# Stage three of a long convolution from cosine and sine sums: four plain float32 matmuls a step in place of twelve float32r ones

## The chip, the cores and the metric

The kernel runs on one core of a Trainium2 chip. The metric is the device time of one execution in microseconds (us); the profile's times are from the first to the last instruction of one profiled execution. The engines are TensorE (PE; PEld are its weight loads), VectorE (DVE), ScalarE (ACT), GpSimd (POOL) and SyncE (SP), which issues most of the DMAs.

## The reference

A gated long convolution and then a feed-forward layer, on 4 sequences of 12480 tokens with 128 channels:

```python
h_mlp = np.maximum(pos_emb @ w1, 0.0) @ w2
h_filt = h_mlp * np.exp(-0.01 * pos)[:, None]
u = x * v
y = irfft(rfft(u, n=2 * S, axis=1) * rfft(h_filt, n=2 * S, axis=0), n=2 * S, axis=1)[:, :S]
a = (x * y).reshape(B * S, D)
h = np.maximum(a @ w_in, 0.0)
out = h * h @ w_out
```

Here S is 12480, B 4, D 128, and the hidden width of the feed-forward layer 2048.

## The kernel before

**The convolution as a two-level transform.** The sequence is padded to 112 x 112 (I = 112) and transformed in two levels with tables of cosines and sines. Stage one multiplies x and v and transforms along the first index for each channel; stage two applies the second level, multiplies with the transform of the filter and keeps the products in W; stage three does the first level of the way back; stage four the second level, multiplies by x and writes the result, transposed, to DRAM (zd), from where the feed-forward layer reads it. W is one SBUF tile of 56 x 512 values a partition: 128 channels, and 4 values for each channel and row pair. Every stage of every batch works in it in place.

**Stage three** runs 64 steps of two channels. In a step, `prep` (L420) casts the pair's 448 values a partition out of W into `vh` as float32r (L424, ScalarE), `prep2` (L427) subtracts it to get the low part `vl` (L431, VectorE), `mm` (L434) makes for each channel k and each part r (real, imaginary) three float32r matmuls through `mm3` (L78 to L80: high x high, high x low, low x high) of 224 columns against the table `ft`, so that r = 0 and r = 1 accumulate into one result, and `evac` (L444) copies the 448 results back into the same channels of W (L445, ScalarE). The table holds the values for an index m and its mirror 111 − m side by side, real and imaginary, split in high and low: 4 x 224 values a partition, loaded by GpSimd's DMA queue (`load_tab`, L84).

**The order of the work** is written out by hand. Each stage is a generator that yields 1, 2 or 3. For batch 0 the stages run by themselves (`big` is true): stage three then prepares two steps ahead and copies back two steps late, and after each step the hook `during` runs one piece of `convert_weights`, which turns 64-bit weights into float32r pairs on VectorE and ScalarE (L113 to L132). For batches 1 to 3 the four stages are one stream, and the feed-forward loop at the end of the kernel advances it: `adv(1)` before its first matmuls, `adv(2)` before ScalarE's work, `adv(3)` after VectorE's. So one step of a stage goes with one feed-forward step f: 6 matmuls into A (L78 to L80), 6 into O for the step before last (`m_o` runs while more than one low part is pending), on ScalarE relu (L686) and square (L693), on VectorE the cast of the square (L700) and the subtraction that gives its low part gl (L705). Every eighth step GpSimd splits a new input (L653).

**Buffers.** PSUM has two pairs of banks A (`psa`), three single banks F (`bank()`, `psf`) and one O. Stage three of batches 1 to 3 takes one F bank a step.

Of the kernel before, what the change touches and what calls it, by code (L numbers as in the profile page):

```python
# [7 lines left out]
F32 = mybir.dt.float32  # L8
F32R = mybir.dt.float32r
# [8 lines left out]
I = 112  # L18
S = I * I
# [3 lines left out]
NP = I // 2  # L23
# [6 lines left out]
HI = I // 2  # L30
# [5 lines left out]
def hyena_moe_kernel(  # L36
# [19 lines left out]
    nc = tc.nc  # L56
# [4 lines left out]
    psa = ctx.enter_context(tc.tile_pool(name="psa", bufs=2, space=bass.MemoryType.PSUM))  # L61
# [3 lines left out]
    W = cpool.tile([KP, NP, 4 * D], F32, name="W")  # L65
# [6 lines left out]
    def bank():  # L72
        return psf.tile([128, 512], F32, tag="F", name="F")

    def mm3(o, L, R, first=True, last=True):
        lh, ll = L
        rh, rl = R
        nc.tensor.matmul(o, lh, rh, start=first, stop=False)  # L78
        nc.tensor.matmul(o, lh, rl, start=False, stop=False)  # L79
        nc.tensor.matmul(o, ll, rh, start=False, stop=last)  # L80

    def load_tab(p, src, k):
        t = p.tile([I, k, 2 * I], F32R, name="tab", bufs=1)
        nc.gpsimd.dma_start(out=t, in_=src)  # L84
        return t

    def convert_weights(p, tp, dst):
        n = 512
# [49 lines left out]
    def by_channel(d0, d1):  # L138
        return W[:I].rearrange("p t (d c) -> p d t c", c=4)[:, d0:d1]
# [199 lines left out]
    def stage2(filt, big, side="left", hook=None):  # L339
# [6 lines left out]
        with pool("s2", side) as p:  # L346
# [51 lines left out]
            for t in range(n + lag):  # L398
# [9 lines left out]
                if hook is not None:  # L408
                    hook(t)

    def stage3(big, ft=None, hook=None):
        n = D // 2
        with pool("s3") as p:
            if ft is None:
                ft = load_tab(p, f_tab, 4)
            q = {}
            pa = 2 if big else 1
            lag = 2 if big else 1

            def prep(t):  # L420
                if t >= n:
                    return
                hi = p.tile([I, 2, NP, 4], F32R, tag="vh", name="vh", bufs=lag + pa)
                nc.scalar.copy(hi, by_channel(2 * t, 2 * t + 2))  # L424
                q[t] = hi

            def prep2(t):  # L427
                if t >= n:
                    return
                lo = p.tile([I, 2, NP, 4], F32R, tag="vl", name="vl", bufs=lag + pa)  # L430
                nc.vector.tensor_sub(out=lo, in0=by_channel(2 * t, 2 * t + 2), in1=q[t].bitcast(F32))  # L431
                q[t] = q[t], lo

            def mm(t):  # L434
                hi, lo = q.pop(t)
                A = bank()
                for k in range(2):
                    o = A[:I, k * 2 * I : (k + 1) * 2 * I]
                    for r in range(2):
                        h, l = (x[:, k].rearrange("p t (k r) -> p (t k) r", r=2)[:, :, r] for x in (hi, lo))  # L440
                        mm3(o, (h, l), (ft[:, 2 * r, :], ft[:, 2 * r + 1, :]), first=r == 0, last=r == 1)
                return A

            def evac(t, A):  # L444
                nc.scalar.copy(by_channel(2 * t, 2 * t + 2), A[:I, : 4 * I].rearrange("p (d t c) -> p d t c", d=2, c=4))  # L445

            if not big:
                yield from rest(2)
            yield 1
            for t in range(pa):  # L450
                prep(t)
            yield 2
            for t in range(pa):
                prep2(t)
            prev = {}
            for t in range(n + lag):
                yield 1
                if t - lag in prev:
                    evac(t - lag, prev.pop(t - lag))
                prep(t + pa)  # L460
                yield 2
                prep2(t + pa)
                yield 3
                if t < n:
                    prev[t] = mm(t)
                if hook is not None:
                    hook(t - n)
# [129 lines left out]
    ftp = take("ftp")  # L597
# [17 lines left out]
    run(s1f)  # L615
    run(s2f)
    s2 = stage2(False, True, "left", lambda t: t % TC == 0 and 3 <= t // TC + 2 < NP // TC and table(t2s, t // TC + 2))
    ft = load_tab(ftp, f_tab, 4)
    run(s1)
    run(s2)  # L620
    held["tbp"].close()
# [138 lines left out]
    for i in range(B * NG):  # L760
        for f in range(NS):
            adv(1)
            A = m_h(zT, f)
            last = m_o(*pend.pop(0)) if len(pend) > 1 else None
# [4 lines left out]
            while len(late) > len(tail):  # L769
                x, y, st = late.pop(0)  # L770
# [17 lines left out]
def _constants():  # L788
    import numpy as np

    def r12(a):
        b = np.ascontiguousarray(a, np.float32).view(np.uint32)
        b = (b + np.uint32(0x7FF) + ((b >> np.uint32(12)) & np.uint32(1))) & np.uint32(0xFFFFF000)
        return b.view(np.float32)

    def split(a):
        hi = r12(a)
        return hi, r12(a - hi.astype(np.float64))

    def split16(a):  # L800
        hi = a.astype(np.float16)
        return hi, (a - hi.astype(np.float64)).astype(np.float16)
# [1 line left out]
    n = np.arange(I)  # L804
    m = np.arange(NP)
# [7 lines left out]

    e_tab = np.stack([e, turned(e), f, turned(f)], 1).astype(np.float32)

    def th(i):
        return 2 * np.pi * (n[:, None] * (2 * i[None] + 1) % (2 * I)) / (2 * I)

    am, ax = th(m), th(I - 1 - m)
    fr = np.stack([-np.sin(ax), np.cos(am), np.cos(ax), -np.sin(am)], 2).reshape(I, -1) / S  # L820
    fi = np.stack([-np.cos(ax), -np.sin(am), -np.sin(ax), -np.cos(am)], 2).reshape(I, -1) / S
    f_tab = np.stack(split(fr) + split(fi), 1)

    k = n[:, None] + I * n[None]
    def angle(at):
# [78 lines left out]
```

## Time and profile before

| what | value |
|---|---|
| median of 3 runs | 3294.92 us (3293.74 to 3298.14) |
| the profiled execution, its own time | 3295.03 us |
| its span, first to last instruction | 3293.2 us |
| mean granted TensorE clock, share of full | 0.993 |
| TensorE busy | 98% of the span |
| VectorE, ScalarE, GpSimd busy | 77%, 74%, 40% |
| matmul instructions | 18294 |
| stage three of batch 0 | 317 to 403 us |
| stage three of batch 1, first to last matmul | 917.3 to 1150.7 us |

Busy shares are means over stages whose limits differ. TensorE's recorded matmul lengths overlap each other; the distance from one to the next is read from the chain of waits. A group of instructions is given with its number, its busy time in us and the mean of one in ns, and then the idle time ahead of it on its engine with what ended it.

### The profile page before, as it was taken

The numbers are of one execution on the slowest core, as the hardware profiler recorded it, in microseconds if no ns is written. First come the engines' busy times: TensorE is split into PE (matmuls) and PEld (weight loads), VectorE is DVE, ScalarE is ACT, GpSimd is POOL, SyncE is SP. The second block draws the span as 40 slices with busy tenths as digits, with TensorE's granted clock in tenths as the row PEclk, the third lists the DMA queues.
The fourth block names the chain that finished last, engine by engine and source line by source line (L and its number), as shares of the span: only waits on it lengthen the run. The fifth ranks groups of instructions, "written<-read, shape, count | busy, mean of one in ns | idle before, by whom it ended". The sixth has DMA issues, their size and how long they took to land.

```text
span 3293.2 us, 53552 instructions
## 1 busy us (share of the span) xinstructions
PE 3215.9 (98%) x18294; PEld 2957.1 (90%) x18294; DVE 2533.9 (77%) x3175; ACT 2449.0 (74%) x3349; POOL 1315.7 (40%) x1425
## 2 busy tenths in 40 slices
PE   8986999999999999999999999999999999999998
PEld 6754999999999999998999999998999999999998
DVE  6459788878866689878876689887876679877776
ACT  4331777777787778777788888778788778888886
POOL 6277065646610056646620056565630046300000
PEclk9999999999999999999999999999999999999999
DMA  5586166434400066434410056433410046300000
GB/s 139 180 209 160 55 149 154 122 97 121 119 22 14 22 153 157 123 98 120 121 35 15 18 133 158 133 97 116 125 52 15 14 105 160 89 26 25 24 23 20
DMA packets 330154, 306.08 MB, mean 93 GB/s; under 512 B 143785, under 2 KB 288025, under 8 KB 329881
## 3 DMA queue, kind: packets, MB, share of 16 engines
q1 hardware_dynamic: 300696, 256.08, 28.4%
q0 software_dynamic: 29184, 46.58, 6.1%
q8 instruction: 145, 2.38, 0.3%
q14 instruction: 129, 1.05, 0.1%
HBM read 216.29 MB, written 63.77 MB: 85 GB/s over the span
## 4 chain that ended last, share of the span: by engine, by line
PE 91%; DVE 3%; DMA 3%; issue 2%; POOL 2%; ACT 1%; SPq 0%; DVEq 0%; POOLq 0%; ACTq 0%
PE A L78 11%; PE A L80 11%; PE A L79 11%; PE O L79 9%; PE O L80 9%; PE O L78 9%; PE F L79 7%; PE F L78 7%; PE F L80 7%; PE F L366 5%; PE F L285 4%; PE A L282 1%; DMA Hd<-he 1%; DMA vt<-vs 1%; POOL W L384 1%
## 5 line engine op out<-in xcount | busy, mean ns | idle before, releaser
L686 ACT ACTIVATE r<-A 128x892 f32<-128x892 f32 x896 | 820.5, 916 | 301.8 <-PE A L80 284.6
L78 PE MATMUL A<-zh,wt 128*128 128x446 f32 x1792 | 702.0, 392 | 0.6 <-DVE gl L705 0.5
L705 DVE TENSOR_TENSOR gl<-r,gh 128x892 fp32r<-128x892 f32 x503 | 613.0, 1219 | 87.0 <-ACT r L693 73.4
L80 PE MATMUL A<-zh,wt 128*128 128x446 f32 x1792 | 653.1, 364 | 0.0
L79 PE MATMUL A<-zl,wt 128*128 128x446 f32 x1792 | 651.6, 364 | 0.0
L689 ACT ACTIVATE gh<-r 128x892 fp32r<-128x892 f32 x512 | 486.2, 950 | 143.1 <-PE O L80 131.0
L653 POOL TENSOR_TENSOR zl<-zi,zh 128x446 fp32r<-128x446 f32 x111 | 131.6, 1185 | 1149.1 <-PE F L80 599.7
L79 PE MATMUL O<-gl,wt 128*128 128x446 f32 x1440 | 524.3, 364 | 1.0 <-DVE gl L705 0.7
L80 PE MATMUL O<-gh,wt 128*128 128x446 f32 x1440 | 523.7, 364 | 0.0
L78 PE MATMUL O<-gh,wt 128*128 128x446 f32 x1440 | 523.0, 363 | 0.0
L700 DVE CAST gh<-r 128x892 fp32r<-128x892 f32 x384 | 242.5, 632 | 358.0 <-ACT r L693 356.7
L693 ACT ACTIVATE r<-r 128x892 f32<-128x892 f32 x504 | 479.3, 951 | 14.5
L705 DVE TENSOR_TENSOR gl<-A,gh 128x892 fp32r<-128x892 f32 x392 | 426.0, 1087 | 74.5 <-ACT gh L689 56.3
L691 DVE SCALAR_TENSOR_TENSOR A<-A,r 128x892 f32<-128x892 f32 x392 | 425.0, 1084 | 56.7 <-ACT r L686 54.5
L78 PEld LDWEIGHTS A<-zh,wt 128*128 128x128 f32 x1792 | 339.1, 189 | 26.3 <-DVE gl L705 2.4
L79 PEld LDWEIGHTS A<-zl,wt 128*128 128x128 f32 x1792 | 340.1, 190 | 19.7 <-DVE zl L653 0.2
L80 PEld LDWEIGHTS A<-zh,wt 128*128 128x128 f32 x1792 | 337.0, 188 | 22.9
L384 POOL TENSOR_TENSOR W<-W,m 112x256 f32<-112x256 f32 x224 | 224.2, 1001 | 214.3 <-DVE m L382 188.2
L507 POOL TENSOR_TENSOR al<-W,ah 112x512 fp32r<-112x512 f32 x212 | 278.9, 1315 | 47.8 <-ACT ah L505 34.4
L79 PEld LDWEIGHTS O<-gl,wt 128*128 128x128 f32 x1440 | 272.1, 189 | 22.6 <-DVE gl L705 3.8
L78 PEld LDWEIGHTS O<-gh,wt 128*128 128x128 f32 x1440 | 271.0, 188 | 18.7
L80 PEld LDWEIGHTS O<-gh,wt 128*128 128x128 f32 x1440 | 269.8, 187 | 18.3
(115 smaller groups left out, 6253.0 us busy)
## 6 DMA issues: line engine op xcount, KB each, us to landing
ht<-Hd SPq DMA_DIRECT2D x224, 224.0 KB
tb<-t POOLq DMA_DIRECT2D x224, 196.0 KB, 3.2
xt<-xs SPq DMA_DIRECT2D x128, 196.0 KB
vt<-vs SPq DMA_DIRECT2D x128, 196.0 KB
xt<-x SPq DMA_DIRECT2D x224, 112.0 KB
out<-ot SPq DMA_DIRECT2D x112, 223.0 KB
tb<-t2s SPq DMA_DIRECT2D x168, 105.0 KB
zd<-zs SPq DMA_DIRECT2D x222, 64.0 KB
```

The source lines that it names most:

```text
L78: nc.tensor.matmul(o, lh, rh, start=first, stop=False)
L79: nc.tensor.matmul(o, lh, rl, start=False, stop=False)
L80: nc.tensor.matmul(o, ll, rh, start=False, stop=last)
L366: nc.tensor.matmul(U[:I, k * 256 : (k + 1) * 256], tb[:, k, :], a[:, k], start=True, stop=True)
L384: nc.gpsimd.tensor_sub(out=re[0], in0=re[0], in1=im[1])
L507: eng.tensor_sub(out=lo, in0=w, in1=hi.bitcast(F32))
L686: nc.scalar.activation(r, h, AF.Relu)
L689: nc.scalar.activation(hi, r, AF.Square)
L691: nc.vector.scalar_tensor_tensor(out=h, in0=h, scalar=0.0, in1=r, op0=ALU.max, op1=ALU.mult)
L693: nc.scalar.activation(r, r, AF.Square)
L700: nc.vector.tensor_copy(hi, g)
L705: nc.vector.tensor_sub(out=lo, in0=g, in1=hi.bitcast(F32))
```

## The change

Only stage three and its table change. The table now holds, for 56 indices m, the cosines and the sines, and a second time both negated: 2 x 112 values a partition in plain float32, loaded by SyncE's queue (`load_f`). `prep` copies the pair's 448 values as plain float32; every third copy goes to GpSimd in batches 1 to 3, every fifth in batch 0, the others to ScalarE. `mm` makes four matmuls of 112 columns, one for each channel and part, each into its own quarter of the 448 results; nothing accumulates. So each channel has four runs of 56 sums: cosines and sines of the real part, and of the imaginary part. In batch 0 two steps share a pair A instead of taking a bank F each. `evac` copies all 448 into a tile `c` on ScalarE; then sums of two runs each (224 values in one instruction on VectorE, one operand in PSUM; in batch 0 every fifth on GpSimd, both from `c`) go to one half of the pair's values in W, and the differences of the same runs (224 values on GpSimd, from `c`) to the other half, for the index and its mirror. The low part, `prep2` and L431 are gone.

```diff
--- before.py
+++ after.py
@@ -78,11 +78,6 @@
         nc.tensor.matmul(o, lh, rh, start=first, stop=False)
         nc.tensor.matmul(o, lh, rl, start=False, stop=False)
         nc.tensor.matmul(o, ll, rh, start=False, stop=last)
-
-    def load_tab(p, src, k):
-        t = p.tile([I, k, 2 * I], F32R, name="tab", bufs=1)
-        nc.gpsimd.dma_start(out=t, in_=src)
-        return t
 
     def convert_weights(p, tp, dst):
         n = 512
@@ -408,41 +403,50 @@
                 if hook is not None:
                     hook(t)
 
+    def load_f(p):
+        ft = p.tile([I, 2, I], F32, name="ft", bufs=1)
+        nc.sync.dma_start(out=ft, in_=f_tab)
+        return ft
+
     def stage3(big, ft=None, hook=None):
         n = D // 2
         with pool("s3") as p:
             if ft is None:
-                ft = load_tab(p, f_tab, 4)
-            q = {}
+                ft = load_f(p)
+            q, two = {}, {}
             pa = 2 if big else 1
             lag = 2 if big else 1
 
             def prep(t):
                 if t >= n:
                     return
-                hi = p.tile([I, 2, NP, 4], F32R, tag="vh", name="vh", bufs=lag + pa)
-                nc.scalar.copy(hi, by_channel(2 * t, 2 * t + 2))
-                q[t] = hi
-
-            def prep2(t):
-                if t >= n:
-                    return
-                lo = p.tile([I, 2, NP, 4], F32R, tag="vl", name="vl", bufs=lag + pa)
-                nc.vector.tensor_sub(out=lo, in0=by_channel(2 * t, 2 * t + 2), in1=q[t].bitcast(F32))
-                q[t] = q[t], lo
+                q[t] = p.tile([I, 2, NP, 4], F32, tag="v", name="v", bufs=lag + pa)
+                (nc.gpsimd.tensor_copy if t % (5 if big else 3) == 2 else nc.scalar.copy)(q[t], by_channel(2 * t, 2 * t + 2))
 
             def mm(t):
-                hi, lo = q.pop(t)
-                A = bank()
+                v = q.pop(t)
+                if big:
+                    if t % 2 == 0:
+                        two[0] = psa.tile([128, 2, 512], F32, tag="A", name="A")
+                    A = two[0][:, t % 2, :]
+                else:
+                    A = bank()
                 for k in range(2):
-                    o = A[:I, k * 2 * I : (k + 1) * 2 * I]
                     for r in range(2):
-                        h, l = (x[:, k].rearrange("p t (k r) -> p (t k) r", r=2)[:, :, r] for x in (hi, lo))
-                        mm3(o, (h, l), (ft[:, 2 * r, :], ft[:, 2 * r + 1, :]), first=r == 0, last=r == 1)
+                        o = A[:I, (2 * k + r) * I : (2 * k + r + 1) * I]
+                        nc.tensor.matmul(o, v[:, k].rearrange("p t (k r) -> p (t k) r", r=2)[:, :, r], ft[:, r, :], start=True, stop=True)
                 return A
 
             def evac(t, A):
-                nc.scalar.copy(by_channel(2 * t, 2 * t + 2), A[:I, : 4 * I].rearrange("p (d t c) -> p d t c", d=2, c=4))
+                q = A[:I, : 4 * I].rearrange("p (d q m) -> p d q m", d=2, q=4)
+                dst = W[:I].rearrange("p m (d a c) -> p a d c m", a=2, c=2)[:, :, 2 * t : 2 * t + 2]
+                c = p.tile([I, 2, 4, HI], F32, tag="c", name="c", bufs=lag + 1)
+                nc.scalar.copy(c, q)
+                if big and t % 5 == 4:
+                    nc.gpsimd.tensor_add(out=dst[:, 0, :, 1::-1], in0=c[:, :, 3:0:-2], in1=c[:, :, 0:3:2])
+                else:
+                    nc.vector.tensor_add(out=dst[:, 0, :, 1::-1], in0=q[:, :, 3:0:-2], in1=c[:, :, 0:3:2])
+                nc.gpsimd.tensor_sub(out=dst[:, 1], in0=c[:, :, 0:3:2], in1=c[:, :, 3:0:-2])
 
             if not big:
                 yield from rest(2)
@@ -450,8 +454,6 @@
             for t in range(pa):
                 prep(t)
             yield 2
-            for t in range(pa):
-                prep2(t)
             prev = {}
             for t in range(n + lag):
                 yield 1
@@ -459,7 +461,6 @@
                     evac(t - lag, prev.pop(t - lag))
                 prep(t + pa)
                 yield 2
-                prep2(t + pa)
                 yield 3
                 if t < n:
                     prev[t] = mm(t)
@@ -615,7 +616,7 @@
     run(s1f)
     run(s2f)
     s2 = stage2(False, True, "left", lambda t: t % TC == 0 and 3 <= t // TC + 2 < NP // TC and table(t2s, t // TC + 2))
-    ft = load_tab(ftp, f_tab, 4)
+    ft = load_f(ftp)
     run(s1)
     run(s2)
     held["tbp"].close()
@@ -788,15 +789,6 @@
 def _constants():
     import numpy as np
 
-    def r12(a):
-        b = np.ascontiguousarray(a, np.float32).view(np.uint32)
-        b = (b + np.uint32(0x7FF) + ((b >> np.uint32(12)) & np.uint32(1))) & np.uint32(0xFFFFF000)
-        return b.view(np.float32)
-
-    def split(a):
-        hi = r12(a)
-        return hi, r12(a - hi.astype(np.float64))
-
     def split16(a):
         hi = a.astype(np.float16)
         return hi, (a - hi.astype(np.float64)).astype(np.float16)
@@ -813,13 +805,9 @@
 
     e_tab = np.stack([e, turned(e), f, turned(f)], 1).astype(np.float32)
 
-    def th(i):
-        return 2 * np.pi * (n[:, None] * (2 * i[None] + 1) % (2 * I)) / (2 * I)
-
-    am, ax = th(m), th(I - 1 - m)
-    fr = np.stack([-np.sin(ax), np.cos(am), np.cos(ax), -np.sin(am)], 2).reshape(I, -1) / S
-    fi = np.stack([-np.cos(ax), -np.sin(am), -np.sin(ax), -np.cos(am)], 2).reshape(I, -1) / S
-    f_tab = np.stack(split(fr) + split(fi), 1)
+    a = 2 * np.pi * (n[:, None] * (2 * m[None] + 1) % (2 * I)) / (2 * I)
+    c, s = np.cos(a) / S, np.sin(a) / S
+    f_tab = np.stack([np.concatenate([c, s], 1), np.concatenate([-c, -s], 1)], 1).astype(np.float32)
 
     k = n[:, None] + I * n[None]
     def angle(at):
```

## Rows read from the trace of the kernel before

**Rows 1.** The page, part 1: busy us (share of the span) xinstructions.
```profile
PE 3215.9 (98%) x18294; PEld 2957.1 (90%) x18294; DVE 2533.9 (77%) x3175; ACT 2449.0 (74%) x3349; POOL 1315.7 (40%) x1425
```

**Rows 2.** Windows, batches 0 and 1: length, busy PE PEld DVE ACT POOL, PEclk, DMA, GB/s.
```profile
317.00:403.00 86.00, 85.04 (x768) 83.50 (x768) 72.20 (x144) 68.47 (x144) 2.90 (x6) 0.97 0.19 55
930.00:1130.00 200.00, 200.00 (x1303) 190.72 (x1302) 128.33 (x163) 160.66 (x231) 8.06 (x7) 1.00 0.05 15
```

**Rows 3.** Chain of waits inside stage three of batch 1: start us, us, what.
```profile
1002.28 0.10 PE F L78
...
1003.55 0.21 PE A L78
...
1005.97 0.10 PE F L78
```

**Rows 4.** Chain of waits inside stages one and two of batch 1.
```profile
601.12 1.52 PE F L285 x8
...
801.87 0.86 PE F L366 x4
```

**Rows 5.** Groups by line and shape, whole span: busy us, mean ns; idle before.
```profile
L80 PEld LDWEIGHTS F<-tab,vl 112*112 112x112 f32 x1024 | 187.3, 183 | 0.2 <-DVE vl L431 0.2
```

**Rows 6.** Timeline of ScalarE, batch 1: start us, us, engine, line, op [idle before].
```profile
...
1003.59 0.54 ACT L445 COPY W<-F 112x448 f32<-112x448 f32 x1 [0.57 <-PE F L80]
1004.02 0.57 ACT L424 CAST vh<-W 112x448 fp32r<-112x448 f32 x1
1004.80 0.92 ACT L686 ACTIVATE r<-A 128x892 f32<-128x892 f32 x1 [0.22 <-PE A L80]
1005.75 0.95 ACT L693 ACTIVATE r<-r 128x892 f32<-128x892 f32 x1
```

**Rows 7.** Groups by line and shape, whole span, nearest prices.
```profile
L535 DVE TENSOR_TENSOR z<-F,xt 112x256 f32<-112x256 f32 x222 | 92.0, 414 | 0.0
...
L268 POOL TENSOR_TENSOR ut<-xt 112x224 f32<-112x224 f32 x126 | 86.4, 685 | 123.7 <-DVE xt L266 72.6 <-PE F L285 46.4
...
L262 POOL TENSOR_TENSOR ut<-W 112x228 f32<-112x228 f32 x23 | 22.3, 970 | 21.3 <-PE A L283 10.5 <-DVE W L193 5.9 <-PE A L282 5.0
...
L494 POOL MEMSET z<- 32x512 f32 x8 | 3.9, 522 | 111.5 <-DVE cv L119 77.7 <-issue 33.8
...
L266 POOL TENSOR_TENSOR xt<-xt,vt 112x448 f32<-112x448 f32 x96 | 110.8, 1154 | 72.5 <-DMA vt<-vs 66.7 <-PE F L285 5.8
```

**Rows 8.** Timeline of VectorE, then GpSimd, 910.5 to 914 us.
```profile
910.69 1.93 DVE L700 CAST gh<-r 128x892 fp32r<-128x892 f32 x1
912.65 1.09 DVE L705 TENSOR_TENSOR gl<-r,gh 128x892 fp32r<-128x892 f32 x1
913.66 0.62 DVE L700 CAST gh<-r 128x892 fp32r<-128x892 f32 x1
...
910.96 1.17 POOL L653 TENSOR_TENSOR zl<-zi,zh 128x446 fp32r<-128x446 f32 x1
```

**Rows 9.** Timeline of GpSimd and VectorE in stage two, batch 0.
```profile
250.38 0.85 POOL L386 TENSOR_TENSOR W<-W,m 112x256 f32<-112x256 f32 x1
250.39 1.12 DVE L386 TENSOR_TENSOR W<-W,m 112x256 f32<-112x256 f32 x1
```

**Rows 10.** One line's instructions: duration ns min/median/max, first and last start.
```profile
L386 DVE TENSOR_TENSOR W<-W,m x16: 425/1118/1125, 231.0 to 315.8; 112x256 f32<-112x256 f32 x16
```

**Rows 11.** Groups by line and shape, 317 to 403 us.
```profile
L132 DVE TENSOR_TENSOR wt<-cv 128x512 fp32r<-128x512 f32 x8 | 5.5, 686 | 0.0
...
L122 ACT CAST cv<-cv 128x512 f32<-128x512 int32 x8 | 5.0, 623 | 11.4 <-DVE cv L119 11.4
...
L113 DVE TENSOR_SCALAR cv<-raw 128x512 int32<-128x512 int32 x8 | 3.4, 420 | 0.0
```

**Rows 12.** Timeline of stage one of the filter.
```profile
61.42 0.55 ACT L294 COPY W<-A 120x448 f32<-120x448 f32 x1 [2.29 <-PE A L283]
61.44 0.97 POOL L262 TENSOR_TENSOR ut<-W 112x228 f32<-112x228 f32 x1 [0.80 <-PE A L283]
```

## The prediction, made before the changed kernel ran

> **What bounds the kernel now.** I read the page's busy times first: TensorE is busy 98% of the span, VectorE and ScalarE about three quarters, GpSimd 40% [rows 1]. A mean says little, so next the windows. Stage three runs four times. For batch 0 it runs by itself with the conversion of the weights beside it, from 317 to 403 us, and TensorE is busy 85.04 of those 86 us. For batches 1 to 3 each of its 64 steps is placed behind one feed-forward step of an earlier batch, and a 200 us window in the middle has TensorE busy for all of 200.00 us [rows 2]. Both forms are bound by TensorE, and so is everything after: what stage three gives back on TensorE is not taken away by another stage, as long as no other engine becomes slower than TensorE inside stage three.
>
> Then the chain of waits, which gives the pace of matmuls better than their recorded lengths (these overlap). One step repeats every 3.69 us (1002.28 to 5.97). Its stage-three block of 12 float32r matmuls takes 1003.55 − 1002.28 = 1.27 us, about 0.105 us for each of 224 columns [rows 3]. The other 2.42 us are 12 feed-forward matmuls.
>
> **TensorE's part of the change.** Each step had 2 channels x 2 parts (real and imaginary) x 3 products = 12 float32r matmuls of 224 columns. It now has 2 x 2 = 4 plain float32 matmuls of 112 columns. The kernel has plain float32 matmuls in stages one and two, so the price can be read there: stage one's four of 224 columns appear as 8 instructions and take 1.52 us, stage two's two of 256 columns appear as 4 and take 0.86 us [rows 4]. So one float32 matmul is two instructions, of 0.190 us for 224 columns and 0.215 us for 256. That is 0.85 and 0.84 ns a column: two 2.4 GHz cycles for each column and instruction. At 112 columns that gives 0.094 us, the lower bound. No row has such short float32 matmuls with a new stationary tile for each. The nearest is today's float32r instruction, which streams as many cycles (224 of one each) behind a weight load of the same 112 columns: 0.105 us, the upper bound among overlapped cases. I take 0.100 us in between: 8 x 0.100 = 0.80 us, against 1.27. That saves 0.47 us a step (0.43 to 0.52), and for 3 x 64 = 192 steps **90 us** (82 to 100).
>
> This needs the weight loads to stay hidden. One recorded load of stage three lasts 183 ns [rows 5], while the matmuls that use them follow each other every 105 ns: loads overlap both the stream before and each other. The page "TensorE: Matmul & The Clock Gate" of the Trainium skill (Part 3, "What overlaps and what doesn't") says that a weight load overlaps a matmul in flight only where the row group differs. Here every load takes the same 112 rows; by that sentence today's block would last 12 x (0.093 + 0.183) = 3.3 us (an estimate), and the trace has 1.27, so here the measurement decides. A milder form of it is the rival on the slow side below.
>
> **Does another engine take over in batches 1 to 3?** The new step of TensorE is 3.69 − 0.47 = 3.22 us.
> ScalarE is busy 160.66 us in 200, that is 2.96 us in each of the 54.2 steps [rows 2]. The cast of a channel pair (0.57 us) becomes a plain copy, and every third goes to GpSimd: −0.19. The copy out of PSUM (0.54 us) stays and now fills a tile instead of W [rows 6]. That makes 2.77 of 3.22 us. It waits 0.57 and 0.22 us in each step today [rows 6], and this waiting shrinks; nothing is released later.
> VectorE loses the subtraction of the low part, and gets the sum: 224 elements, one operand in PSUM. The nearest row is a product of 256 elements with one operand in PSUM, 414 ns [rows 7]; I take 0.38. With the feed-forward's cast of 0.62 and subtraction of 1.09 [rows 8] this is 2.1 us.
> GpSimd, nearly idle here (8.06 us in 200), gets the difference of 224 elements in each step and a copy of 448 in every third. The difference reads contiguous rows and writes with a long stride. A contiguous sum of 224 takes 685 ns, one of 228 that reads with a long stride 970 [rows 7]; I take 0.77. No row has a one-input copy on GpSimd: a memset of 512 (522 ns) bounds it below, a product of 448 (1154 ns) above [rows 7]; I take 0.70. The page "GPSIMD Engine Reference" (section 3.1) of the Trainium skill gives 1.03 cycles an element for such bodies, an estimate of 0.38 us for 448 elements; by it the sum on GpSimd below would be 0.1 us a step less, and no run so far shows it. With the split of the feed-forward's input (1.17 us in every eighth step [rows 8]) GpSimd has 0.77 + 0.23 + 0.15 = 1.15 us a step.
>
> These two disturb each other. A VectorE sum with both operands in SBUF takes 1.12 us when GpSimd is at work and 0.425 at best [rows 9, 10], and the feed-forward's cast took 1.93 instead of 0.62 us while GpSimd worked, ending half a microsecond after GpSimd did [rows 8]. So a GpSimd instruction can keep VectorE waiting to its end. If every GpSimd microsecond stopped VectorE, VectorE would need 2.1 + 1.15 = 3.25 us, just TensorE's 3.22. Some of it falls on the new sum, which reads PSUM, or where VectorE waits for ScalarE's square anyway. A late low part costs nothing at first: the second matmuls use it two steps later. I therefore take no loss, with a thin margin; the second case below prices its absence.
>
> **Batch 0 alone.** Today 86 us. TensorE would need 64 x 0.80 = 51 us, so it is no longer the bound. ScalarE: copies out every 0.43 us, copies in every 0.56 [rows 6], four of five here: 64 x 0.88 = 56 us, and 16 casts of the conversion, 10 us [rows 11]: 66 us. GpSimd: 64 x 0.77, and a copy and a sum in every fifth step (13 x 1.5): 69 us. VectorE: 51 sums of 0.38 and the conversion's 6 instructions of 0.42 and 4 of 0.69 for each of 8 pieces [rows 11], 42 us: 61 us. Taken apart these give 69 us; that is the lower bound. If GpSimd and the conversion's VectorE instructions exclude each other throughout, it is 69 + 42 = 111 us, the upper bound. TensorE may also start an even step only when the sum of three steps earlier has freed its PSUM pair. Near the middle, nearer the low end because the sums read PSUM: 84 us, a gain of **2 us** (−25 to +17).
>
> **What costs nothing.** The table goes from GpSimd's queue to SyncE's, 4 issues, and shrinks to a quarter; two steps without matmuls of stage three (7 us) cover it, and what stands behind it on SyncE is wanted steps later. In SP's queue it passes only loads made well ahead. The last difference of each stage three must land before stage four's first cast, where only a copy had to: under 1 us for batch 0, and for the others stage four begins with an empty step. PSUM: one bank a step is still released three steps later. ScalarE's new copy of a pair does not wait for the sums being written into other channels of W: in stage one a GpSimd sum read W's channels from 61.44 us while ScalarE wrote others from 61.42 [rows 12].
>
> **Sum.** The profiled execution took 3295.03 us (span 3293.2, 1.8 around it), 0.1 above the median. 3295.0 − 90 − 2 = **3203 us**.
>
> **The rivals.**
> (a) GpSimd and VectorE become the bound. With the difference at 0.97 and the copy at 1.15 us, GpSimd has 0.97 + 0.38 + 0.15 = 1.5 us a step, and where all of it stops VectorE, 3.6 us: only 0.09 a step is left of the gain, 17 us, and batch 0 at 105 us gives 19 back: 3297. Half of this, the likelier form, is a step of 3.42 and batch 0 at 95: −52 + 9, 3252. For it: the 1.93 us cast. Against it: VectorE is busy 128.33 us in 200 today [rows 2], 2.37 of 3.69 us in a step, and the change leaves it 2.1.
> (b) Slower: the loads of these short matmuls set the pace. If a load is not overlapped with the next one, eight of 0.183 us make 1.46 us, 0.19 more than today: +36 us, and batch 0 at 64 x 1.46 = 94 us, +8: 3339. It decides from 0.158 us an instruction (1.27 / 8) on. For it: the load is recorded at 183 ns, and plain float32 has not been seen with a stream so short. Against it: 1024 loads for each of the three products, hidden at 105 ns [rows 3, 5].
> (c) The copy of a pair waits for the sums through W after all. ScalarE then adds a GpSimd difference to two steps of three: 2.77 + 0.5 = 3.3 us, and batch 0 at 100: −75 + 14, 3234. Against it rows 12.
>
> **Chances.** Forecast 0.72 (own range 3180 to 3225), (a) 0.17, mostly its half form, (b) 0.06, (c) 0.05. From no change, 0.2% is 6.6 us and about what a measurement can tell: faster takes the forecast, (c) and most of (a): 0.91; the extreme of (a) gives same 0.03; slower is (b). The range goes from 3178 (0.094 us and a short batch 0) to 3255, which holds the half form of (a) and (c).
>
> **What would show it.** Right: float32 blocks of 8 instructions near 0.80 us in the chain, a step of 3.2 us with TensorE busy throughout in batches 1 to 3; batch 0 between 69 and 100 us with TensorE no longer full. Wrong: TensorE waiting on gl or on v in stage three, casts of the feed-forward near 1.9 us in every step, or float32 instructions 0.15 us apart.

## The result, and the profile after

The changed kernel takes 3219.61 us (median; 3218.82 to 3225.78), the kernel before 3294.33 us on the same chip: a ratio of 0.9776, 95% interval 0.9759 to 0.9793. That is 75 us faster, where 92 were forecast.

The page, part 1, of the changed kernel, which answers to [rows 1]:

```profile
PE 3109.4 (97%) x17270; PEld 2850.4 (89%) x17270; DVE 2556.1 (79%) x3163; ACT 2412.2 (75%) x3273; POOL 1707.7 (53%) x1765
```

TensorE has 1024 instructions fewer (12 became 8 in each of 256 steps) and is still busy 97% of a shorter span. GpSimd went from 40 to 53%. The windows answer to [rows 2]; columns are the length, the busy time of PE, PEld, DVE, ACT and POOL, PEclk, the DMA share and GB/s. First stage three of batch 0, then a stretch of stage three of batch 1:

```profile
315.00:415.00 100.00, 68.88 (x512) 63.91 (x512) 70.24 (x131) 64.71 (x132) 83.87 (x93) 0.88 0.17 49
...
940.00:1140.00 200.00, 200.00 (x1226) 189.59 (x1225) 153.66 (x186) 170.94 (x240) 109.80 (x94) 1.00 0.08 22
```

In batch 1 TensorE is busy for all of 200.00 us, as before. In batch 0 it is busy 68.88 us of 100, and no engine is full: GpSimd has 83.87, VectorE 70.24, ScalarE 64.71. The chain of waits of batch 1 (start, length, what) answers to [rows 3]:

```profile
1002.67 0.82 PE F L437 x8
1003.50 0.22 PE A L78
...
1005.92 0.82 PE F L437 x8
```

The step lasts 1005.92 − 1002.67 = 3.25 us, where it was 3.69, and its block of eight float32 instructions takes 0.83 us up to the next matmul, where twelve float32r ones took 1.27.

Where the 76 us of span went (3293.2 to 3217.1) follows from the first and last moments of each stage three. From its first matmul to the first cast of stage four:

| stage three | before, us | changed, us | difference |
|---|---|---|---|
| batch 0 | 317.6 to 403.2, 85.6 | 315.6 to 414.6, 99.0 | +13.4 |
| batch 1 | 917.3 to 1156.8, 239.5 | 927.8 to 1139.3, 211.5 | −28.0 |
| batch 2 | 1670.6 to 1910.1, 239.5 | 1651.9 to 1863.4, 211.5 | −28.0 |
| batch 3 | 2426.1 to 2667.2, 241.1 | 2379.3 to 2591.3, 212.0 | −29.1 |

The sum is −71.7; batch 0 starts its stage 2.0 us earlier (in runs with the same code up to there this start lies between 314.2 and 319.5 us, so it is scatter), and the rest, 2.4 us, is spread. So batches 1 to 3 gave 85 us, close to the forecast 90, and batch 0 took 13 back, where a gain of 2 was forecast.

What stretched in batch 0 is in the groups by line and shape from 315 to 415 us (busy us, mean ns of one, idle before):

```profile
L449 POOL TENSOR_TENSOR W<-c 112x224 f32<-112x224 f32 x64 | 62.9, 1005 | 14.5 <-ACT c L444 14.0
...
L127 DVE TENSOR_TENSOR wt<-cv 128x512 fp32r<-128x512 f32 x8 | 6.4, 800 | 0.1
...
L109 DVE TENSOR_SCALAR cv<-cv 128x512 f32<-128x512 f32 x8 | 6.3, 790 | 0.3
...
L108 DVE TENSOR_SCALAR cv<-raw 128x512 int32<-128x512 int32 x7 | 3.1, 437 | 0.0
```

GpSimd's difference takes 1005 ns in the mean. Of the conversion's instructions (their lines moved up by five) L109 took 427 ns in the kernel before:

```profile
L114 DVE TENSOR_SCALAR cv<-cv 128x512 f32<-128x512 f32 x8 | 3.4, 427 | 0.3
```

It now takes 790, and L127 800, where [rows 11] have 686; L108 is near the 420 of [rows 11]. These are mutual delays, as in [rows 8, 9]. But it was not clear that they set the length of the stage: the waits of the same stretch (who waited for whom: us in total, times, longest) run through all engines:

```profile
DVE W L448 <- ACT c L444: 27.4, 26, 3.3
PE A L437 <- DVE W L448: 17.6, 17, 2.2
...
PEld A L437 <- POOL v L424: 10.7, 10, 2.7
PE A L437 <- POOL v L424: 8.8, 10, 2.5
ACT cv L117 <- DVE cv L114: 8.7, 8, 1.9
...
ACT c L444 <- POOL W L449: 6.9, 8, 2.1
...
ACT c L444 <- DVE W L448: 5.9, 15, 0.9
```

### The profile page after: what moved, and what is told of

It is laid out like the page before. It is cut to its first block, busy times and chain, and to the rows that moved or that the text cites. A ratio compares the mean times of both kernels' runs of the same rounds, so it can differ in the third digit from the quotient of the medians.

```text
span 3217.1 us, 51651 instructions
## 1 busy us (share of the span) xinstructions
PE 3109.4 (97%) x17270; PEld 2850.4 (89%) x17270; DVE 2556.1 (79%) x3163; ACT 2412.2 (75%) x3273; POOL 1707.7 (53%) x1765
## 4 chain that ended last, share of the span: by engine, by line
PE 89%; POOL 3%; DVE 3%; issue 2%; DMA 2%; ACT 1%; SPq 0%; DVEq 0%; POOLq 0%; ACTq 0%
PE A L78 11%; PE A L80 11%; PE A L79 11%; PE O L79 9%; PE O L80 9%; PE O L78 9%; PE F L361 5%; PE F L437 5%; PE F L280 5%; PE F L79 4%; PE F L78 4%; PE F L80 4%; PE A L277 1%; DMA vt<-vs 1%; POOL W L449 1%
## 5 line engine op out<-in xcount | busy, mean ns | idle before, releaser
L706 DVE TENSOR_TENSOR gl<-r,gh 128x892 fp32r<-128x892 f32 x503 | 628.3, 1249 | 87.2 <-ACT r L694 73.6
L706 DVE TENSOR_TENSOR gl<-A,gh 128x892 fp32r<-128x892 f32 x392 | 426.0, 1087 | 73.6 <-ACT gh L690 55.6
L449 POOL TENSOR_TENSOR W<-c 112x224 f32<-112x224 f32 x256 | 329.9, 1294 | 289.1 <-ACT c L444 288.5
L379 POOL TENSOR_TENSOR W<-W,m 112x256 f32<-112x256 f32 x224 | 217.0, 969 | 211.0 <-DVE m L377 185.1
L78 PEld LDWEIGHTS O<-gh,wt 128*128 128x128 f32 x1440 | 270.4, 188 | 18.4
```

The source lines that it names most:

```text
L379: nc.gpsimd.tensor_sub(out=re[0], in0=re[0], in1=im[1])
L449: nc.gpsimd.tensor_sub(out=dst[:, 1], in0=c[:, :, 0:3:2], in1=c[:, :, 3:0:-2])
L706: nc.vector.tensor_sub(out=lo, in0=g, in1=hi.bitcast(F32))
```

## The experiments

Two theories for batch 0. **A**: GpSimd and VectorE keep each other out, and GpSimd, with the most work, sets the length. **B**: the in-order engines wait for each other around a ring, with too few buffers between them: a PSUM pair is free again only after VectorE's sum of three steps earlier, VectorE's sum waits for ScalarE's copy, ScalarE's conversion cast waits for VectorE. For batches 1 to 3 the theory is that TensorE alone counts.

### Do the two parts add up?

The old stage for batch 0, the new one for the others (both tables are loaded):

```diff
-    run(stage3(True, ft, during))
+    run(stage3_old(True, ft, during))
```

> Stage three of batch 0 as in the kernel before (float32r, twelve matmuls a step), batches 1 to 3 as in the changed kernel. My theory: the two parts do not touch each other; the changed kernel's stage three of batch 0 takes 99 us where the old one took 86, and batches 1 to 3 give 85 us by TensorE alone. So 3220 - 13 = 3207 us (3202 to 3212). Rival: the loss in batch 0 is made up later by the stream (then 3220, no change), or the old stage costs its 2 us earlier start as well (3209).

Measured: 3208.49 us (ratio to before 0.9735, 0.9719 to 0.9751), with batch 0 at 85.5 us. The mirror, only batch 0 new:

```diff
-    ... ("s3", stage3(False)), ...
+    ... ("s3", stage3_old(False)), ...
```

> The mirror of the run with the old stage in batch 0: batch 0 as changed, batches 1 to 3 as before. My theory (the parts add up): 3295 + 11 = 3306 us (3302 to 3310), slower than before the change. Rival (the loss of batch 0 shows only beside the faster batches): 3295.

Measured: 3309.24 us, ratio 1.0036 (1.0021 to 1.0052): batch 0 lasts 99.0 us here too, and that part of the change alone makes the kernel slower. The parts add up: −88.0 in the first run, +12.7 in this one, together −75.3, where the whole change gave −74.7.

### Have the other engines room in batches 1 to 3?

```diff
-    (nc.gpsimd.tensor_copy if t % (5 if big else 3) == 2 else nc.scalar.copy)(q[t], ...)
+    (nc.gpsimd.tensor_copy if big and t % 5 == 2 else nc.scalar.copy)(q[t], ...)
```

> The changed kernel with all copies of batches 1 to 3 on ScalarE, none on GpSimd. If TensorE bounds these batches and the other engines have room (ScalarE 2.77 of 3.25 us a step, with all copies 2.96), nothing changes: 3217 to 3223. If ScalarE is nearly the bound and the share given to GpSimd carries part of the gain: 5 to 20 us more, 3225 to 3240. If GpSimd's copies hold VectorE up enough to cost time: 3205 to 3215.

Measured: 3223.18 us (3222.50 to 3226.06), 0.2 us above the range of the first case, ratio 0.9780 (0.9763 to 0.9796) beside the changed kernel's 0.9776: no difference that the intervals show. The window of the same stretch:

```profile
940.00:1140.00 200.00, 200.00 (x1229) 189.61 (x1229) 154.73 (x186) 179.77 (x259) 94.10 (x74) 1.00 0.07 20
```

ScalarE is at 179.77 of 200 us and TensorE is still full. GpSimd's third of the copies is not needed for the gain.

### What sets the pace of a short float32 instruction?

Two kernels leave work out in batches 1 to 3, and each was timed in one execution. The first multiplies with 56 of the 112 columns alone (cosine sums stand in for the sine sums; `evac` copies each run of 56 sums twice, so the other engines handle as many elements as before; HI is 56):

```diff
-                        o = A[:I, (2 * k + r) * I : (2 * k + r + 1) * I]
-                        nc.tensor.matmul(o, ..., ft[:, r, :], ...)
+                        w = I if big else HI
+                        o = A[:I, (2 * k + r) * w : (2 * k + r + 1) * w]
+                        nc.tensor.matmul(o, ..., ft[:, r, :w], ...)
```

> Batches 1 to 3 multiply with the first half of the table alone (the 56 cosine columns; the sine sums are left out and the cosine sums used in their place), everything else as in the changed kernel. It asks what sets 0.1025 us for a float32 instruction of 112 columns, where its stream of 224 cycles takes 0.093. If the weight load sets the pace: the block of 8 stays at 0.75 to 0.82 us and the time at 3210 to 3220. If the stream does: the block falls to 0.41 to 0.50 us, the step to 2.85 to 2.95, and the time by 60 to 75 us to 3145 to 3160, with ScalarE then nearly full.

Measured: 3223.97 us, 4 us above the range given for the weight load, with the block as that case has it. The second also loads 64 columns of the stationary tile instead of 112, so rows 64 to 111 of the result are missing (and `evac` works on 64 partitions):

```diff
-                        o = A[:I, (2 * k + r) * I : (2 * k + r + 1) * I]
-                        nc.tensor.matmul(o, v[:, k]...[:, :, r], ft[:, r, :], ...)
+                        w = I if big else HI
+                        g = I if big else 64
+                        o = A[:g, (2 * k + r) * w : (2 * k + r + 1) * w]
+                        nc.tensor.matmul(o, v[:, k]...[:, :g, r], ft[:, r, :w], ...)
```

> As the run with half of the table's columns, and the stationary tile holds 64 of the 112 rows alone (rows 64 to 111 are left out and stay unchanged in W). There the block of 8 stayed at 0.77 us though the stream was halved. If the length of the weight load sets the pace: the block falls to 0.40 to 0.55 us, the step to about 2.95 us, and the time to 3150 to 3175, as far as ScalarE lets it. If each float32 instruction costs about 0.1 us whatever it loads: 0.77 us again and 3224.

Measured: 3222.36 us, which missed both: the block is shorter and the time is the same. Timelines of TensorE (start, length, what; a merged row's length runs to the end of the last). The changed kernel, the last matmul ahead of the block, the block, and two behind it; then the loads (PEld) of the block from the second on:

```profile
1002.31 0.37 PE L80 MATMUL O<-gh,wt 128*128 128x446 f32 x1
1002.51 0.98 PE L437 MATMUL F<-ft,v 112*112 112x112 f32 x8
1003.26 0.45 PE L78 MATMUL A<-zh,wt 128*128 128x446 f32 x1
1003.55 0.36 PE L79 MATMUL A<-zl,wt 128*128 128x446 f32 x1
```

```profile
1002.51 0.80 PEld L437 LDWEIGHTS F<-ft,v 112*112 112x112 f32 x7
```

With half of the columns:

```profile
1004.28 0.37 PE L80 MATMUL O<-gh,wt 128*128 128x446 f32 x1
...
1004.48 0.94 PE L438 MATMUL F<-ft,v 112*112 112x56 f32 x8
...
1005.24 0.45 PE L78 MATMUL A<-zh,wt 128*128 128x446 f32 x1
...
1005.52 0.36 PE L79 MATMUL A<-zl,wt 128*128 128x446 f32 x1
```

```profile
1004.49 0.80 PEld L438 LDWEIGHTS F<-ft,v 112*112 112x112 f32 x7
```

With half of the columns and 64 columns loaded:

```profile
1003.89 0.37 PE L80 MATMUL O<-gh,wt 128*128 128x446 f32 x1
...
1004.19 0.56 PEld L439 LDWEIGHTS F<-ft,v 112*64 112x64 f32 x8 [0.31 <-ACT r L696]
1004.19 0.69 PE L439 MATMUL F<-ft,v 112*64 112x56 f32 x8
...
1004.81 0.47 PE L78 MATMUL A<-zh,wt 128*128 128x446 f32 x1
...
1005.11 0.36 PE L79 MATMUL A<-zl,wt 128*128 128x446 f32 x1
```

From the first start in the block to the first start behind it: 0.75 us, 0.76 and 0.62. This distance is not eight times the pace, because the matmul behind the block starts early and then lasts longer (0.45 us where others have 0.36). The loads give the pace: one lasts 182 ns, so from load to load it is (0.80 − 0.18) / 6 = 0.103 us, with 112 columns streamed and with 56 alike. Half of the stream changes nothing, so the stream is not what these instructions wait for. With 64 columns loaded (138 ns each) it is (0.56 − 0.14) / 7 = 0.060 us. That is 0.92 and 0.94 ns for each column loaded: the load sets the pace inside the block, as the first case had it.

The time did not follow because the ends of the block take back what its inside gives. From its first start to its last the block shrinks from 0.71 to 0.47 us (merged length less one matmul of 0.27 or 0.22). But its first instruction starts 0.30 us after the last matmul ahead of it, not 0.20, since its load (1004.19) does not start ahead of time as the 112-column load does (in the changed kernel at 1002.31, 0.20 us ahead of its matmul); and the matmul behind the block starts 0.15 us after the block's last one, not 0.04. From the last matmul ahead of the block to the second behind it are 1.24, 1.24 and 1.22 us, and the step stays at 3.24 us. Why the 64-column load is not started early is open: the row names a wait for ScalarE, but in 25 of 61 steps the profile finds no releaser for the same 0.31 us.

### Batch 0: how much is the conversion, how much the depth?

The conversion after the stage instead of beside it:

```diff
     def during(t):
-        step(conv)
         if t == -12:
             step(s4)
```

> Changed kernel, but in batch 0 the conversion of the weights runs after stage three instead of beside it. Theory A (GpSimd and the conversion's VectorE instructions keep each other out): the mean of GpSimd's differences in batch 0 falls from 1.0 to 0.75 us or less and the stage from 99 to 65 to 75 us, then the conversion alone adds 45 to 60 us; the total is 3235 to 3250. Theory B (few buffers and the order of the instructions): the stage stays at 90 us or more and the total goes above 3255.

Measured: 3242.88 us. The last difference starts at 390.0 us, so the stage lasts 75 us (from 314.9; to its last difference the changed kernel's has 98.3); the conversion alone then holds stage four until 435.2. The difference (groups, 315 to 415 us):

```profile
L449 POOL TENSOR_TENSOR W<-c 112x224 f32<-112x224 f32 x64 | 42.9, 682 | 18.0 <-ACT c L444 18.0
```

It takes 682 ns, where beside the conversion it took 1005. So the mutual delay is real and theory A passes here, while theory B's 90 us or more failed: without the conversion the same shallow buffers pass in 75 us. This kernel was timed in one execution, and it takes away two things together, the mutual delay and the conversion's place in the ring. Next, deeper buffers with the engines' work unchanged:

```diff
-            pa = 2 if big else 1
-            lag = 2 if big else 1
+            pa = 3 if big else 1
+            lag = 3 if big else 1
...
-                    if t % 2 == 0:
+                    if t % 3 == 0:
                         two[0] = psa.tile([128, 2, 512], F32, tag="A", name="A")
-                    A = two[0][:, t % 2, :]
+                    A = two[0][:, t % 3, :] if t % 3 < 2 else bank()
...
-                c = p.tile([I, 2, 4, HI], F32, tag="c", name="c", bufs=lag + 1)
+                c = p.tile([I, 2, 4, HI], F32, tag="c", name="c", bufs=lag + 2)
```

> Changed kernel with deeper buffers in batch 0's stage three alone: copies three steps ahead, results taken three steps late, nine matmul results in PSUM's pairs and single banks where four were, five tiles c where three were. Theory A (GpSimd and VectorE keep each other out, GpSimd the longest): 97 to 100 us for the stage, total within 3 us of 3220. Theory B (the pair of PSUM banks freed too late and the engines in lockstep): the stage falls to 75 to 90 us, total 3197 to 3211.

Measured: 3209.99 us, ratio 0.9739 (0.9724 to 0.9753), and the stage takes 87.5 us (317.1 to 404.6). Theory A had said no change. That 11.5 us are more than scatter: the five kernels whose batch 0 is that of the changed kernel have 99.0 to 99.6 us. TensorE's wait for VectorE's sum, 17.6 us before, is at 3.0:

```profile
L437 PE MATMUL A<-ft,v 112*112 112x112 f32 x344 | 49.1, 306 | 18.1 <-POOL v L424 9.1 <-ACT v L424 5.8 <-DVE W L448 3.0
```

The window:

```profile
317.00:404.00 87.00, 67.56 (x512) 65.04 (x512) 73.99 (x130) 62.31 (x131) 80.67 (x92) 0.85 0.19 56
```

Now GpSimd is busy 80.67 of 87 us, so A might hold from here on. The next run takes GpSimd's copies and sums away from it:

```diff
-    (nc.gpsimd.tensor_copy if t % (5 if big else 3) == 2 else nc.scalar.copy)(q[t], ...)
+    (nc.gpsimd.tensor_copy if not big and t % 3 == 2 else nc.scalar.copy)(q[t], ...)
...
-                if big and t % 5 == 4:
-                    nc.gpsimd.tensor_add(out=..., in0=c[:, :, 3:0:-2], in1=c[:, :, 0:3:2])
-                else:
-                    nc.vector.tensor_add(out=..., in0=q[:, :, 3:0:-2], in1=c[:, :, 0:3:2])
+                nc.vector.tensor_add(out=..., in0=q[:, :, 3:0:-2], in1=c[:, :, 0:3:2])
```

> The run with deeper buffers, and in batch 0 GpSimd keeps the 64 differences alone: its 13 copies go to ScalarE and its 12 sums to VectorE. Theory A (with buffers deep enough GpSimd, 82 of 87 us busy and kept out by the conversion's VectorE instructions, is what bounds the stage): the stage falls to 72 to 80 us and the time to 3195 to 3203. Theory B (ScalarE's and VectorE's waiting for each other through the conversion bounds it): both get more work, the stage stays at 86 to 92 us, 3209 to 3215.

Measured: 3209.38 us, ratio 0.9735 (0.9720 to 0.9749), stage 86.2 us. GpSimd lost 25 instructions and the stage 1.3 us: theory A, that GpSimd's work sets the length, fails here. The window shows no engine at its limit:

```profile
315.00:403.00 88.00, 65.64 (x514) 63.03 (x514) 71.31 (x145) 69.40 (x146) 71.01 (x70) 0.87 0.19 55
```

TensorE's wait for VectorE's sum is back where it was, in a stage that is no longer for it. So the total of one wait does not tell the length:

```profile
PE A L437 <- DVE W L445: 17.6, 14, 2.2
```

Then the ring itself. The conversion's two ScalarE casts are issued one step later:

```diff
-            nc.scalar.copy(mag, rest)
             yield
+            nc.scalar.copy(mag, rest)
             tf = top.bitcast(F32)
             V.tensor_scalar(out=sgn, in0=top, ...)
-            nc.scalar.copy(hi12, tf)
             yield
+            nc.scalar.copy(hi12, tf)
```

> The run with deeper buffers and GpSimd at the differences alone, and the conversion issues its two ScalarE casts one step later, behind the next step's copies. There no engine of batch 0's stage three was above 82% busy in 86 us. Theory B (in-order waits around a ring: ScalarE's cast waits for VectorE's conversion, which stands behind sums that wait for ScalarE's copies): ScalarE's 7.7 us of waiting for VectorE's conversion go, the stage falls to 76 to 82 us, the time to 3199 to 3206. Theory A (GpSimd and VectorE keep each other out on SBUF, whatever the order): 85 to 88 us, 3207 to 3212.

Measured: 3205.80 us (3205.65 to 3208.59), ratio 0.9733 (0.9716 to 0.9749), stage 82.8 us (317.0 to 399.8), just outside the 76 to 82 expected. The wait that was meant is gone; first the run before this one, then this one:

```profile
ACT cv L117 <- DVE cv L114: 7.7, 7, 1.8
```

```profile
ACT cv L118 <- DVE cv L114: 1.3, 2, 0.7
```

6.4 us of waiting less, 3.4 us of stage: the rest came back as other waits. The whole times of these two runs do not tell them apart (the intervals of the ratios overlap); the 3.4 us rest on one profile of each. And one thing moved that neither theory names, TensorE's granted clock, here 0.96 of full in the stage and 0.87 in the run before:

```profile
315.00:401.00 86.00, 59.39 (x513) 56.20 (x513) 73.14 (x146) 69.20 (x146) 69.34 (x71) 0.96 0.20 57
```

A block of the stage, first of the run before, where the granted clock is 0.50 (1.2 GHz), then of this run, where it is 1.00 (2.4 GHz):

```profile
354.98 1.70 PE L437 MATMUL F<-ft,v 112*112 112x112 f32 x8
```

```profile
354.99 0.99 PE L437 MATMUL F<-ft,v 112*112 112x112 f32 x8
```

How much of the 3.4 us is the clock is not shown. Against the clock as the cause of the changed kernel's 99.0 us stands the run with the copies of batches 1 to 3 on ScalarE: its batch 0 is the same, had a lower clock (0.84 where the changed kernel had 0.88), and lasted 99.0 us too:

```profile
316.00:416.00 100.00, 71.23 (x512) 66.14 (x512) 69.97 (x131) 64.62 (x133) 83.66 (x94) 0.84 0.17 49
```

The same edit on the changed kernel as it is, without the depth:

> The changed kernel with the two casts one step later and nothing else: copies and results two steps apart as they were, GpSimd with its share of copies and sums. Theory B: about 9 us of the 99 come back, 3209 to 3214. If only the depth of the buffers matters: 97 to 100 us, 3217 to 3222.

Measured: 3213.18 us, ratio 0.9754 (0.9739 to 0.9768); stage four starts at 410.6 instead of 414.6 us. The time is in theory B's range, though the interval of its ratio overlaps the changed kernel's, and the stage itself shrank from 99.0 to 96.4 us only, less than the 9 us of waiting that were meant to come back: without depth other waits of the ring take most of its place. Last, on the run with deeper buffers and late casts, GpSimd idle in that stage:

```diff
-                nc.gpsimd.tensor_sub(out=dst[:, 1], in0=c[:, :, 0:3:2], in1=c[:, :, 3:0:-2])
+                if big:
+                    nc.vector.tensor_sub(out=dst[:, 1], in0=q[:, :, 0:3:2], in1=c[:, :, 3:0:-2])
+                else:
+                    nc.gpsimd.tensor_sub(out=dst[:, 1], in0=c[:, :, 0:3:2], in1=c[:, :, 3:0:-2])
```

> The run with deeper buffers and late casts, and in batch 0 the differences move from GpSimd to VectorE as well, with one operand in PSUM like the sums, so GpSimd has nothing in that stage. It prices the exclusion. With GpSimd idle the conversion's VectorE instructions should fall back to 0.42 and 0.69 us, from up to 0.79 and 0.74. Theory B: VectorE gets 64 x 0.45 us more and gives some 6 us back, which makes it the bound: 88 to 95 us for the stage, 3210 to 3218. If the exclusion were the larger cost (theory A): 80 us or less, 3203 or less.

Measured: 3217.90 us, ratio 0.9765 (0.9748 to 0.9781), stage 94.4 us (316.6 to 411.0). The groups of that stretch:

```profile
L447 DVE TENSOR_TENSOR W<-A,c 112x224 f32<-112x224 f32 x43 | 23.3, 541 | 0.0
...
L127 DVE TENSOR_TENSOR wt<-cv 128x512 fp32r<-128x512 f32 x8 | 5.4, 673 | 0.0
...
L109 DVE TENSOR_SCALAR cv<-cv 128x512 f32<-128x512 f32 x8 | 3.9, 492 | 0.3
...
L112 DVE TENSOR_SCALAR cv<-raw 128x512 int32<-128x512 int32 x8 | 3.3, 411 | 0.0
```

Without GpSimd the conversion's instructions are back to 673, 492 and 411 ns: in the run with late casts and GpSimd at the differences they were 737, 793 and 702. Summed over its ten instructions in eight pieces the conversion takes 42.1 us of VectorE here and 48.8 there, so the exclusion costs VectorE about 7 us. The 64 differences cost it 35 (0.54 us each) once GpSimd doesn't do them. GpSimd's help is worth more than it disturbs, and theory A as it was put, GpSimd setting the length, is out.

## Why the prediction came out as it did

The direction, the place and the main mechanism were right. Of the 17 us between 3203 and 3220 batch 0 makes 15 and TensorE's part in the other batches 5 more; some 4 us outside stage three go the other way.

**TensorE's part.** The forecast block was 0.80 us and the step 3.22; the chain shows 0.83 and 3.25. So 0.44 us a step instead of 0.47, and 192 steps give 84.5 us instead of 90, which is what batches 1 to 3 lost together (85.1). The mis-sized term is the price of one float32 instruction, 0.104 us (0.83 / 8) where 0.100 was taken: it came out at the upper bound, that of the float32r instruction behind the same load (0.105 us). The lower bound was made from the stream, and the stream is not what limits it: the loads of 112 columns follow each other every 0.103 us, whether 112 columns are streamed or 56.

**The weight loads.** They overlap here too: 0.103 us from load to load, with loads recorded at 182 ns. Rival (b), loads that do not overlap, did not happen, though overlapping loads do set the pace. The sentence of the page "TensorE: Matmul & The Clock Gate" (Part 3) of the Trainium skill on loads in the same row group does not describe them, as the prediction held from [rows 3, 5].

**The other engines in batches 1 to 3.** No loss, as forecast, but on prices that were too low, which is luck in part: the sum takes 0.66 us (taken 0.38), the difference 1.41 in the mean (taken 0.77), GpSimd's copy 0.77 in the mean and 0.55 at best (taken 0.70). The estimate of 0.38 us from the page "GPSIMD Engine Reference" (section 3.1) of the Trainium skill lies below every copy here; the measurement decides. The groups of the 200 us window show them:

```profile
L449 POOL TENSOR_TENSOR W<-c 112x224 f32<-112x224 f32 x60 | 84.5, 1409 | 79.2 <-ACT c L444 79.2
L706 DVE TENSOR_TENSOR gl<-r,gh 128x892 fp32r<-128x892 f32 x62 | 79.1, 1275 | 2.1
...
L448 DVE TENSOR_TENSOR W<-F,c 112x224 f32<-112x224 f32 x61 | 40.2, 660 | 0.0
L701 DVE CAST gh<-r 128x892 fp32r<-128x892 f32 x61 | 38.6, 633 | 44.1 <-ACT r L694 43.2
...
L424 POOL COPY v<-W 112x448 f32<-112x448 f32 x20 | 15.4, 772 | 0.0
```

The feed-forward's cast is at 633 ns, so the 1.93 us that spoke for rival (a) did not become the rule: GpSimd's difference falls beside the subtraction (L706) that comes after the cast. A timeline of VectorE and then GpSimd:

```profile
1003.43 0.62 DVE L701 CAST gh<-r 128x892 fp32r<-128x892 f32 x1 [0.40 <-ACT r L694]
1004.09 1.09 DVE L706 TENSOR_TENSOR gl<-r,gh 128x892 fp32r<-128x892 f32 x1
```

```profile
1004.25 1.52 POOL L449 TENSOR_TENSOR W<-c 112x224 f32<-112x224 f32 x1 [2.64 <-ACT c L444]
```

Here it is GpSimd that takes 1.52 us instead of 0.68, and VectorE's 1.09 is what it was; in the mean the subtraction takes 1275 ns, where the same stage of the kernel before has 1196. With 153.66 us in 200 VectorE needs 2.5 us of a step's 3.25, where 2.1 had been added up. Rival (a) did not happen in these batches, since VectorE still had room, and moving the copies to ScalarE changed nothing.

**Batch 0** is the step that failed: "84 us, a gain of 2 us". It measured 99.0, a loss of 13.4. That this lies inside the stated 69 to 111 us is luck: those bounds were made from the engines' own times and one interaction between them, the exclusion. (The 0.56 us for a copy in, part of ScalarE's sum, stands in no row of [rows 6], which has 0.57; the sum of 56 us becomes 57 with it.) What the working left out is the depth of the buffers. Deeper buffers alone take 11.5 us off with the same work on every engine, moving work away from GpSimd after that 1.3, and the conversion's casts one step later 3.4 more, some of which may be the clock. How much of the 82.8 us that are left is the exclusion is not priced: with the conversion out of the way, and so the exclusion and the casts together, the stage took 75 us at the old depth. The forecast had the wait in one sentence ("TensorE may also start an even step only when the sum of three steps earlier has freed its PSUM pair") and gave it no price. In the trace it is PE A <- DVE W L448, 17.6 us, and it went with the deeper buffers; as it came back in the next run without making the stage longer, which link of the ring carried the 11.5 us stays open.

**What costs nothing.** Right: the table's move shows in no wait, and the first cast of stage four waits 0.8 us for the last difference in batch 0. Rival (c) did not happen: ScalarE's copies of a pair wait for W once, at the start of batch 0's stage, as in the kernel before.

**The version that beats both kernels** is the changed one with batch 0 one step deeper, GpSimd at the differences alone there, and the casts one step later: 3205.8 us, 14 below the changed kernel. The old batch 0 stage beside the new batches gives 3208.5; the intervals of the two overlap.

## What to carry to other kernels

A change that pays where TensorE is the bound can cost where it is not: price each place of use by itself, and expect the place that stops being bound by TensorE to show the waits that TensorE hid. Where several in-order engines pass each step on to each other and none is above 85% busy, count the buffers between them and look for one engine's instruction that waits for another's from the same step, before moving work about. For short float32 matmuls behind a fresh stationary tile, price the columns that are loaded as well as those that are streamed: here the loads set the pace.

## What the runs showed of the hardware

- A float32 matmul of 112 columns behind its own 112-column weight load is two instructions, and their loads start 0.103 us apart; with 56 columns streamed it is the same. A matmul with fewer columns than its load has gains nothing here.
- With 64 columns loaded instead of 112 it is 0.060 us, so 0.92 and 0.94 ns for each column loaded. But the block's first load no longer starts ahead of the running matmul, the matmul behind the block starts later as well, and the step stays at 3.24 us.
- In batch 0, where TensorE waits for others, its granted clock was 0.88 in the changed kernel and 0.97 in the kernel before; a block of eight of these instructions is recorded at 1.70 us at the lower level and 0.99 at the higher.
- Beside the conversion, GpSimd's difference of 224 elements goes from 0.68 to 1.0 us, in batches 1 to 3, where it falls beside the feed-forward's subtractions, to 1.4 in the mean; VectorE's single-input instruction L109 from 0.43 to 0.79.
